# A third score bank for batch 0, its bias added by TensorE, and one maximum per bank

## The chip, the cores and the metric

The kernel runs on one core of a Trainium2 chip. The metric is device time in microseconds (us) from the start to the end of one execution. The core's engines are TensorE (PE, with its weight loads shown apart as PEld), VectorE (DVE), ScalarE (ACT), GpSimd (POOL) and SyncE (SP), whose queue issues all the DMAs here.

## The reference, cut to what matters

Three layers follow one another for 4 batches of 576 positions: windowed attention with a distance bias, and two gated layers with short convolutions. The change touches only the scores, the bias and the maximum of the attention.

```python
def _attn_ref(q, k, v):                      # 4 batches, 8 heads, 576 positions, 64 wide
    scores = scale * np.matmul(q, k.transpose(0, 1, 3, 2))
    rel = pos[:, None] - pos[None, :]
    bias = slopes[:, None, None] * (-np.abs(rel).astype(np.float32))[None, :, :]
    mask = (rel >= 0) & (rel < window)       # window 128
    scores = np.where(mask, scores + bias[None], -1000000000.0)
    scores = scores - np.max(scores, axis=-1, keepdims=True)
    attn = np.exp(scores)
    attn = attn / (np.sum(attn, axis=-1, keepdims=True) + 1e-09)
    return np.matmul(attn, v).astype(np.float32)

h = np.maximum(x @ w_in, 0.0)                # first gated layer
...
return (h * gate @ w_out)
...
val = x @ w_val                              # second gated layer
return (gate * val @ w_out)
```

## The kernel before

**Work units.** Each batch is cut into two units, u = 0 (positions 0 to 255) and u = 1 (256 to 575). For a unit the four head pairs p go through `attention`, and then `hidden` (weights `win`), `mixed` (`wout`), `valued` (`wval`) and `output` (`wo`) follow on all of the unit's columns. Every weight is kept as a high and a low part, and a dense product is three matmuls (L691, L692, L693).

**Attention of one pair.** Its query blocks of 64 positions are taken in groups of two (u = 1 ends with a group of one). A group owns one bank of the ring `pss`. TensorE writes the scores (L546); VectorE, per block, adds the bias `bm` in place, scales by -0.125 and keeps the minimum (L550, a custom instruction and a second one that reads its accumulator); ScalarE takes exp with that minimum as bias (L558) and its sum; POOL or VectorE adds 1e-9 to the sum (L561, L563), VectorE takes the reciprocal (L568). In batch 0 (`TURN = 1`) a diagonal matrix `dg` is then made (L576, L577), TensorE transposes and scales the exponentials with it back into the same bank (L584), ScalarE and VectorE copy them out in a high and a low half (L590, L592), and only then is the bank free. The product with v goes to the one bank `psx` (L651) and is copied out to x (L667, L672). `vscale` uses `psx` too (L464, L478).

**Banks.** `pss` has three banks, but `ps_s.spare = (20,)` keeps the third out of the ring for its first 20 groups, which are exactly batch 0's (4 x 2 and 4 x 3). In that time the third bank takes the fillers.

**Weights.** The four weights come in 24 pieces of 128 x 512, in the order in, out, val, o2, through a ring of three raw buffers. A piece costs two passes of ScalarE (L390, L392), two of VectorE (L394, L403), a cast by ScalarE or POOL (L409, L410) and a subtraction by POOL (L368). All of it runs in the first 100 us, beside batch 0's attention.

**Order.** A planner places all operations on the engines by priorities and assumed costs, seven passes, and keeps the shortest; engines then run their lists strictly in that order. So a change of a cost or of a ring changes the order of everything behind it. Where the plan leaves TensorE free for over 250 ns, `warm` puts fillers (L858), bf16 matmuls of zeros, until the plan's first use of the third `pss` bank.

Of the kernel before, what the change touches and what calls it, by code (L numbers as in the profile page):

```python
# [11 lines left out]
BF16 = mybir.dt.bfloat16  # L12
# [12 lines left out]
RAWS = 3  # L25
TURN = 1
RW = 2 * WC

# [216 lines left out]
def attention_moe_moe_kernel(  # L245
# [25 lines left out]
    def st(name, shape, dt):  # L271
        return sb.tile(shape, dt, name=name)
# [20 lines left out]
    bm = st("bm", [128, NP, 192], BF16)  # L293
    idle = st("idle", [128, 256], BF16)

# [24 lines left out]
    ps_s = Ring("pss", 3, [128, 512], F32, ps)  # L320
    ps_s.spare = (20,)
    ring_pw = Ring("pm", 0, None, None)
# [167 lines left out]
    def attention(b, u, p, prio, step):  # L490
# [44 lines left out]
        for gi, g in enumerate(groups):  # L535
# [8 lines left out]

            def scores(blk=blk):
                return [nc.tensor.matmul(out=o, lhsT=q_t[:, i, :], rhs=k_t[:, kc:kc + nkey], start=True, stop=True,  # L546
                                         skip_group_check=True) for i, o, nkey, kc in blk]
            pg.add("PE", sum(mm4_t(b_[2]) for b_ in blk), scores, pr, (qk,), ((sk, 0), (sk, 1)))
            for i, s, nkey, _ in blk:
                pg.add("DVE", 128 + 1.05 * nkey, lambda i=i, s=s, nkey=nkey: nc.vector.tensor_tensor_reduce(  # L550
                    out=s, in0=s, in1=bm[:, p, 192 - nkey:192], op0=ALU.add, op1=ALU.min,
                    scale=-0.125, scalar=3.0e38, accum_out=stt[:, 0, i:i + 1]), pr, ("bm",), ((sk, i - a), (stk, 0, i)), bank=sk)
            for i, s, nkey, _ in blk:
                to, tok = s, ()
                if turn:
                    c0 = 256 * i + 128 * (j0 + i < 2) + 64 * ((j0 + i) % 2 and j0 + i > 1)
                    to, tok = pe_[:, c0:c0 + nkey], ((pk, 0, i),)
                pg.add("ACT", act_t(nkey, True, 2), lambda i=i, s=s, to=to: nc.scalar.activation(  # L558
                    out=to, in_=s, func=AF.Exp, scale=-1.0, bias=stt[:, 0, i:i + 1],
                    accum_out=stt[:, 1, i:i + 1]), pr, ((stk, 0, i), "pz" + pk[1:]), ((sk, i - a), (stk, 1, i)) + tok, bank=sk)  # L560
# [236 lines left out]
    def zeros(wide, prio):  # L797

        for i, t in enumerate(ring_p.t):
            flat = t.rearrange("p q a c -> p (q a c)").bitcast(F32) if wide else t.rearrange("p q a c -> p q (a c)")  # L800
            for a, e in ((192, 384), (704, 832), (1216, 1280)):
                z = flat[:, a:e] if wide else flat[:, :, a:e]
                pg.add("POOL", 60 + (e - a) * 1.7, lambda z=z: nc.gpsimd.memset(z, 0.0), prio, (),
                       (f"pz{i}",) + tuple((f"p{i}", q, g) for q in range(2) for g in range(5)))

    zeros(TURN > 0, -1e6)
    for i, t in enumerate(ring_sg.t):
        pg.add("DVE", 200, lambda t=t: nc.vector.memset(t, 0), -2e6, (), (f"sg{i}",))
    sync(lambda: nc.sync.dma_start(out=eye, in_=ident), -1e6, (), ("eye",), 182.0)
    pg.add("POOL", 200, lambda: nc.gpsimd.memset(one, 1.0), -1e6, (), ("one",))  # L810
# [32 lines left out]
    for i, (b, u) in enumerate(todo):  # L843
# [3 lines left out]
        if i + 1 < len(todo):  # L847
# [5 lines left out]
            attentions(b2, u2, base + (9588.0 if (b, u) == (0, 0) else 0.0), t - base)  # L853
    order = pg.order()
    def warm(t, end):

        while t + 250.0 < end:
            nc.tensor.matmul(out=ps_s.t[-1][:, 0:256], lhsT=idle[:, 0:128], rhs=idle, start=True, stop=True,  # L858
                             skip_group_check=True)
            t += 125.0 if t > 940.0 + 3600.0 else 220.0  # L860

    first = next((o.start for o in order if o.eng == "PE" and any(k[0] == ps_s.name + "2" for k in o.wkeys)), 0.0)
# [68 lines left out]
```

## Time and profile before

| | |
|---|---|
| Time before, median of 3 runs | 455.79 us (453.82 to 456.14) |
| The profiled execution's own time | 454.31 us |
| Its span in the trace | 452.5 us |
| TensorE busy | 436.9 us, 97% |
| VectorE, ScalarE, POOL busy | 342.7, 319.9 and 201.9 us |
| DMA | 57.85 MB, mean 128 GB/s |

Busy times are sums over instructions, and instructions of one engine can overlap; fillers count as busy for TensorE. The time of an execution is some 1.8 us longer than the span of its trace. The share of the whole hides two stages: before about 90 us the weights are made ready and fillers run, and behind it there are none.

### The profile page before, as it was taken

The page shows a single profiled execution, that of the slowest core. Times are in us where ns is not written, and L with a number is a line of the kernel's source. Part 1 is how long each engine was busy: PE and PEld are TensorE (multiplying, and loading weights), DVE is VectorE, ACT ScalarE, POOL GpSimd, SP SyncE. Part 2 cuts the span into 40 slices and gives each one's busy share as a digit, 9 for nine tenths or more (in the row PEclk, how much of TensorE's full clock was granted, in tenths as well). Part 3 has the DMA queues.
Part 4 walks back from the last instruction along what each step waited for, and adds up shares of the span by engine and source line. Part 5 has one row for each costly group of instructions (what it writes and reads, how often), then busy time and mean ns, then how long its engine had stood idle before and what let it go on. Part 6 is the DMA issues. An engine that isn't in the chain of part 4 may idle for free.

```text
span 452.5 us, 10277 instructions
## 1 busy us (share of the span) xinstructions
PE 436.9 (97%) x3605; PEld 412.1 (91%) x3605; DVE 342.7 (76%) x1056; ACT 319.9 (71%) x930; POOL 201.9 (45%) x341
## 2 busy tenths in 40 slices
PE   7988999999999999999999999999999999999997
PEld 5667888899999999999999999998999998998996
DVE  5799988998977558995969479967979487917390
ACT  2799999964867668785974578677956576847442
POOL 1477898881553327030560436041722164454511
PEclk9999999999999999999999999999999999999999
DMA  8665757557264525658441527395352429350001
GB/s 268 221 233 198 236 171 236 178 183 250 81 100 99 129 67 114 163 128 173 132 81 49 110 77 134 103 189 138 63 112 67 128 64 170 90 119 1 0 1 59
DMA packets 75235, 57.85 MB, mean 128 GB/s; under 512 B 55984, under 2 KB 65968, under 8 KB 75184
## 3 DMA queue, kind: packets, MB, share of 16 engines
q1 hardware_dynamic: 75184, 57.21, 48.6%
q8 instruction: 28, 0.46, 0.4%
q14 instruction: 23, 0.19, 0.1%
HBM read 39.10 MB, written 4.72 MB: 97 GB/s over the span
## 4 chain that ended last, share of the span: by engine, by line
PE 59%; DVE 15%; ACT 13%; DMA 7%; issue 4%; POOL 1%; SPq 0%; DVEq 0%; ACTq 0%; POOLq 0%
PE pm L691 17%; PE pm L692 15%; PE pm L693 15%; PE pss L546 5%; DVE gts L353 4%; PE psx L651 4%; DMA pt<-p 3%; DVE t L353 2%; ACT sg L390 2%; DMA raw<-in_w_in 2%; DVE pss L550 1%; ACT pss L558 1%; PE pss L584 1%; ACT pm L392 1%; DMA raw<-in_w_val 1%
## 5 line engine op out<-in xcount | busy, mean ns | idle before, releaser
L691 PE MATMUL pm<-x,win 128*128 128x256 f32 (+1 forms) x256 | 80.9, 316 | 2.1 <-DVE t L353 2.0
L691 PE MATMUL pm<-g,wout 128*128 128x254 f32 (+1 forms) x256 | 79.8, 312 | 0.2
L692 PE MATMUL pm<-g,wout 128*128 128x254 f32 (+1 forms) x256 | 76.1, 297 | 0.0
L692 PE MATMUL pm<-x,win 128*128 128x256 f32 (+1 forms) x256 | 76.0, 297 | 0.0
L693 PE MATMUL pm<-x,win 128*128 128x256 f32 (+1 forms) x256 | 75.8, 296 | 0.0
L693 PE MATMUL pm<-g,wout 128*128 128x254 f32 (+1 forms) x256 | 75.7, 296 | 0.0
L353 DVE SCALAR_TENSOR_TENSOR t<-pm,cc,t 128x325 f32<-128x325 f32 (+3 forms) x112 | 56.1, 513 | 15.1 <-ACT t L346 11.9
L368 POOL TENSOR_TENSOR g<-t,g 128x254 fp32r<-128x254 f32 (+1 forms) x64 | 51.9, 814 | 28.2 <-ACT g L337 25.5
L546 PE MATMUL pss<-qk 128*128 128x192 f32 (+2 forms) x288 | 57.5, 322 | 3.9 <-DVE pt L592 3.0
L550 DVE CUSTOM_DVE_ANT_0 pss<-pss,bm 128x192 f32<-128x192 f32 (+2 forms) x144 | 47.9, 339 | 14.9 <-PE pss L546 12.9
L563 POOL TENSOR_SCALAR st<-st 128x2 f32<-128x2 f32 (+1 forms) x56 | 11.1, 199 | 103.6 <-ACT pss L558 87.8
L353 DVE SCALAR_TENSOR_TENSOR gts<-pm,cc,gts 128x322 f32<-128x322 f32 (+4 forms) x120 | 57.2, 506 | 0.1
L558 ACT ACTIVATE pss<-pss,st 128x192 f32<-128x192 f32 (+2 forms) x108 | 40.7, 377 | 17.2 <-DVE st L550 15.8
L691 PEld LDWEIGHTS pm<-x,win 128*128 128x128 f32 x256 | 48.2, 188 | 5.0 <-DVE t L353 3.4
L546 PEld LDWEIGHTS pss<-qk 128*128 128x128 f32 x288 | 44.3, 192 | 7.4 <-DVE pt L592 5.7
L691 PEld LDWEIGHTS pm<-g,wout 128*128 128x128 f32 x256 | 48.2, 188 | 1.6 <-ACT pm L392 0.3
L692 PEld LDWEIGHTS pm<-g,wout 128*128 128x128 f32 x256 | 48.5, 190 | 0.0
L693 PEld LDWEIGHTS pm<-g,wout 128*128 128x128 f32 x256 | 48.5, 190 | 0.0
L692 PEld LDWEIGHTS pm<-x,win 128*128 128x128 f32 x256 | 48.3, 189 | 0.0
L693 PEld LDWEIGHTS pm<-x,win 128*128 128x128 f32 x256 | 48.2, 188 | 0.0
L611 DVE SCALAR_TENSOR_TENSOR p<-pss,st,p 128x192 f16<-128x192 f32 (+1 forms) x103 | 36.4, 386 | 12.8 <-DMA pt<-p 9.0
L609 ACT ACTIVATE p<-pss,st 128x192 f16<-128x192 f32 (+1 forms) x103 | 35.9, 403 | 14.0 <-DMA pt<-p 10.2
(109 smaller groups left out, 1172.4 us busy)
## 6 DMA issues: line engine op xcount, KB each, us to landing
qk<-in_qk SPq DMA_DIRECT2D x16, 544.0 KB, 3.7
qk<-in_qk SPq DMA_DIRECT2D x16, 384.0 KB, 3.5
raw<-in_w_out SPq DMA_DIRECT2D x12, 512.0 KB, 4.0
vr<-in_vN SPq DMA_DIRECT2D x16, 256.0 KB, 3.0
raw<-in_w_in SPq DMA_DIRECT2D x8, 512.0 KB, 3.9
raw<-in_vN SPq DMA_DIRECT2D x8, 384.0 KB, 4.4
out<-t SPq DMA_DIRECT2D x16, 161.0 KB, 1.9
raw<-in_w_val SPq DMA_DIRECT2D x4, 512.0 KB, 3.5
```

The lines of the kernel that those rows point to most:

```text
L353: pg.add("DVE", dve_t(n, 0 if isinstance(scalar, float) else 1), lambda: nc.vector.scalar_tensor_tensor(out=out, in0=in0, scalar=scalar, i ...
L368: "POOL": (pool_t(n, True), lambda: nc.gpsimd.tensor_tensor(out=lo, in0=src, in1=hi.bitcast(F32), op=ALU.subtract))}
L546: return [nc.tensor.matmul(out=o, lhsT=q_t[:, i, :], rhs=k_t[:, kc:kc + nkey], start=True, stop=True, skip_group_check=True) for i, o, nke ...
L550: pg.add("DVE", 128 + 1.05 * nkey, lambda i=i, s=s, nkey=nkey: nc.vector.tensor_tensor_reduce(out=s, in0=s, in1=bm[:, p, 192 - nkey:192], ...
L558: pg.add("ACT", act_t(nkey, True, 2), lambda i=i, s=s, to=to: nc.scalar.activation(out=to, in_=s, func=AF.Exp, scale=-1.0, bias=stt[:, 0, ...
L563: "POOL": (165, lambda a=a, e=e: nc.gpsimd.tensor_scalar(stt[:, 2, a:e], stt[:, 1, a:e], 1e-9, 1.0 / PSC, op0=ALU.add, op1=ALU.mult))}
L609: pg.add("ACT", act_t(nkey, True, 1), lambda i=i, s=s, hi=hi: nc.scalar.activation(out=hi, in_=s, func=AF.Copy, scale=stt[:, 2, i:i + 1]), ...
L611: pg.add("DVE", dve_t(nkey, 1), lambda i=i, s=s, hi=hi, lo=lo: nc.vector.scalar_tensor_tensor(out=lo, in0=s, scalar=stt[:, 2, i:i + 1], in ...
L651: r.append(nc.tensor.matmul(out=oap, lhsT=lhs, rhs=rhs, start=(i == first[h]), stop=(i == last[h]), skip_group_check=True))
L691: return [nc.tensor.matmul(out=o, lhsT=wh, rhs=hi, start=first, stop=False), nc.tensor.matmul(out=o, lhsT=wh, rhs=lo, start=False, stop=Fa ...
L692: nc.tensor.matmul(out=o, lhsT=wh, rhs=lo, start=False, stop=False),
L693: nc.tensor.matmul(out=o, lhsT=wl, rhs=hi, start=False, stop=last)]
```

## The change

Batch 0 (`BIASED`) gets the third score bank. TensorE adds the bias itself: behind each score matmul one of the bf16 identity `eyeb` with `bm`, into the same columns. VectorE takes one maximum over a group's bank (two when its blocks differ in width), and a tiny instruction on VectorE or POOL multiplies it by -0.125. `eyeb` is a copy of `eye` by ScalarE. The fillers, now 192 columns wide, go to columns 320 to 511 of `psx`, and accumulate there; they are placed up to 80 us of the plan.

```diff
+FILL = 80000.0
+BIASED = (0,)
...
-    idle = st("idle", [128, 256], BF16)
+    idle = st("idle", [128, 128], BF16)
+    eyeb = st("eyeb", [128, 128], BF16)
...
-    ps_s.spare = (20,)
...
+                for i, o, nkey, kc in blk:
+                    r.append(nc.tensor.matmul(out=o, lhsT=q_t[:, i, :], rhs=k_t[:, kc:kc + nkey], start=True, stop=not biased,
+                                              skip_group_check=True))
+                    if biased:
+                        r.append(nc.tensor.matmul(out=o, lhsT=eyeb, rhs=bm[:, p, 192 - nkey:192], start=False, stop=True,
+                                                  skip_group_check=True))
...
+            pg.add("PE", sum(mm4_t(b_[2]) + biased * (30 + b_[2] / 2.4) for b_ in blk), scores, pr,
+                   (qk,) + (("bm", "eyeb") if biased else ()), ((sk, 0), (sk, 1)))
+            if biased:
+                same = len({nkey for _, _, nkey, _ in blk}) == 1
+                for bs in ([blk] if same else [[x] for x in blk]):
...
+                    pg.add("DVE", 68 + 1.1 * nkey * nbl, lambda src=src, i0=i0, nbl=nbl: nc.vector.tensor_reduce(
+                        out=stt[:, 0, i0:i0 + nbl], in_=src, axis=mybir.AxisListType.X, op=ALU.max), pr,
+                        ((sk, 0), (sk, 1)), ((stk, 3, i0),), bank=sk)
+                pg.add(("DVE", "POOL"), (75, 165), (
+                    lambda a=a, e=e: nc.vector.tensor_scalar(stt[:, 0, a:e], stt[:, 0, a:e], -0.125, 0.0, op0=ALU.mult, op1=ALU.add),
...
-            for i, s, nkey, _ in blk:
+            for i, s, nkey, _ in () if biased else blk:
...
+    sync(lambda: nc.sync.dma_start(out=eye, in_=ident), -1e6, (), ("eye",), 182.0)
     zeros(TURN > 0, -1e6)
+    pg.add("ACT", 220, lambda: nc.scalar.activation(out=eyeb, in_=eye, func=AF.Copy), -1e6, ("eye",), ("eyeb",))
...
         while t + 250.0 < end:
-            nc.tensor.matmul(out=ps_s.t[-1][:, 0:256], lhsT=idle[:, 0:128], rhs=idle, start=True, stop=True,
+            nc.tensor.matmul(out=ps_x.t[0][:, 320:512], lhsT=idle[:, 0:128], rhs=bass.AP(idle.tensor, idle.offset, [list(idle.ap[0]), [0, 2], [1, 96]]), start=not filled, stop=True,
                              skip_group_check=True)
...
-                if o.start < first:
+                if o.start < FILL:
```

The program's first scores on TensorE, before (`qk` holds a pair's queries and keys, `idle` the zeros of the fillers):

```order
L546 MATMUL pss_125<-qk_105 128x64
L546 MATMUL pss_125<-qk_105 128x128
L546 MATMUL pss_126<-qk_105 128x192 x2
L858 LDWEIGHTS idle
L858 MATMUL pss_127<-idle 128x256
```

and in the changed kernel, whose lines have moved by a few numbers:

```order
L552 MATMUL pss_126<-qk_106 128x64
L555 LDWEIGHTS eyeb
L555 MATMUL pss_126<-bm,eyeb 128x64
L552 MATMUL pss_126<-qk_106 128x128
L555 LDWEIGHTS eyeb
L555 MATMUL pss_126<-bm,eyeb 128x128
L552 MATMUL pss_127<-qk_106 128x192
```

Each score block has a weight load and a matmul behind it, 36 times in all. A little further on in the changed kernel, with what an instruction waits for:

```order
L466 MATMUL psx_129<-eye,vmx 4x128 [waits DMAHW2_49,Pool_49]
L607 MATMUL pss_126<-dg_117,p_116 128x128 [waits Activation_49,Pool_49]
L607 MATMUL pss_126<-dg_118,p_116 128x128 [waits DVE_49]
L886 LDWEIGHTS idle
L886 MATMUL psx_129<-idle 128x192 [waits DVE_49]
L886 LDWEIGHTS idle
L886 MATMUL psx_129<-idle 128x192
```

The first of this block of eleven fillers now waits for VectorE, which reads `psx` behind L466; before, fillers waited for nothing but `idle`. There are six such blocks, with 57 of the 121 fillers. The third place is the last dense work ahead of the first matmul with `wo`, before (`wval` is the weight of `valued`, `g` its moving operand):

```order
L584 MATMUL pss_126<-dg_117,p_115 128x128 x2
L584 MATMUL pss_126<-dg_118,p_115 128x128 x2
L691 MATMUL pm_122<-g_87,wval_65 128x254
L692 MATMUL pm_122<-g_87,wval_65 128x254
L693 MATMUL pm_122<-g_87,wval_66 128x254
```

and in the changed kernel:

```order
L714 MATMUL pm_123<-g_80,wval_65 128x254
L715 MATMUL pm_123<-g_80,wval_65 128x254
L716 MATMUL pm_123<-g_80,wval_66 128x254
L552 MATMUL pss_126<-qk_106 128x64
L552 MATMUL pss_126<-qk_106 128x128
L714 MATMUL pm_123<-g_88,wval_65 128x254
```

Before, batch 0's transposes still stand there; in the changed kernel they are done, and scores of batch 1 stand in their place.

## Rows read from the trace of the kernel before

**Rows 1.** The page: span, and busy time of each engine.
```profile
span 452.5 us, 10277 instructions
PE 436.9 (97%) x3605; PEld 412.1 (91%) x3605; DVE 342.7 (76%) x1056; ACT 319.9 (71%) x930; POOL 201.9 (45%) x341
```

**Rows 2.** Five stretches: length, busy us of each engine, PE clock, DMA share, GB/s.
```profile
0.00:15.00 15.00, 12.00 (x81) 9.74 (x82) 9.32 (x36) 4.93 (x18) 2.81 (x15) 1.00 0.77 256
15.00:30.00 15.00, 12.84 (x110) 9.84 (x109) 11.61 (x37) 13.71 (x39) 10.42 (x18) 1.00 0.69 223
30.00:75.00 45.00, 41.73 (x351) 35.56 (x348) 42.02 (x113) 42.81 (x108) 38.29 (x56) 1.00 0.64 209
75.00:90.00 15.00, 14.39 (x142) 13.73 (x140) 13.69 (x36) 14.77 (x37) 13.31 (x18) 1.00 0.61 202
90.00:452.50 362.50, 355.89 (x2930) 343.27 (x2930) 266.02 (x837) 243.69 (x732) 137.10 (x237) 1.00 0.45 105
```

**Rows 3.** Stretches again, the fillers (L858) alone: PE, PEld, clock.
```profile
0.00:30.00 30.00, 13.08 (x93) 9.36 (x93) 1.00 0.73 240
30.00:75.00 45.00, 11.86 (x96) 9.03 (x93) 1.00 0.64 209
```

**Rows 4.** Waits up to 95 us: total us, times, longest.
```profile
PEld pss L546 <- DVE pt L592: 5.7, 10, 1.6
```

**Rows 5.** Timeline near the start: start, duration, engine, line.
```profile
1.66 0.42 SPq L809 DMA_DIRECT2D eye<-in_ident  x1
...
5.56 0.23 DVE L550 CUSTOM_DVE_ANT_0 pss<-pss,bm 128x64 f32<-128x64 f32 x1 [3.48 <-PE pss L546]
```

**Rows 6.** VectorE's groups by shape up to 100 us: busy us, mean ns.
```profile
L550 DVE CUSTOM_DVE_ANT_0 pss<-pss,bm 128x192 f32<-128x192 f32 x27 | 9.7, 358 | 0.3
L550 DVE DVE_READ_ACCUMULATOR2_ANT st<- 128x1 f32 x35 | 4.9, 141 | 0.0
L444 DVE TENSOR_REDUCE vmx<-raw 128x2 f32<-128x768 f32 x3 | 2.8, 936 | 0.0
L444 DVE TENSOR_REDUCE vmx<-gts 128x4 f32<-128x1024 f32 x1 | 1.2, 1219 | 0.3 <-DMA gts<-in_vN 0.3
L466 DVE TENSOR_REDUCE vst<-psx 4x1 f32<-4x128 f32 x2 | 0.5, 272 | 0.0
```

**Rows 7.** Timeline of VectorE from 24 us, one group's blocks and the next.
```profile
24.11 0.35 DVE L550 CUSTOM_DVE_ANT_0 pss<-pss,bm 128x192 f32<-128x192 f32 x1
...
24.84 0.26 DVE L550 CUSTOM_DVE_ANT_0 pss<-pss,bm 128x64 f32<-128x64 f32 x1
...
25.41 0.68 DVE L403 SCALAR_TENSOR_TENSOR gts<-raw,pm 128x512 uint32<-128x512 uint32 x1
```

**Rows 8.** Timeline of TensorE, twelve fillers in a row.
```profile
25.16 1.48 PE L858 MATMUL pss<-idle 128*128 128x256 bf16 x12
```

**Rows 9.** ScalarE's groups by shape up to 100 us.
```profile
L558 ACT ACTIVATE p<-pss,st 128x192 f32<-128x192 f32 x27 | 11.1, 418 | 1.5 <-DVE st L550 1.5
L590 ACT ACTIVATE pt<-pss 128x512 f16<-128x512 f32 x11 | 6.5, 594 | 3.5 <-PE pss L584 3.5
L409 ACT ACTIVATE wo<-gts 128x512 fp32r<-128x512 f32 x3 | 1.9, 631 | 0.1
```

**Rows 10.** Timeline: the last piece of `wo` on POOL, its first matmul on TensorE.
```profile
97.43 1.28 POOL L368 TENSOR_TENSOR wo<-gts,wo 128x512 fp32r<-128x512 f32 x1
...
99.48 0.28 PE L691 MATMUL pm<-g,wo 128*128 128x254 f32 x1
```

**Rows 11.** Timeline of TensorE: transposes, scores and products with v one behind another.
```profile
88.43 0.61 PE L584 MATMUL pss<-dg,p 128*128 128x128 f32 x4
...
88.87 0.61 PE L546 MATMUL pss<-qk 128*128 128x64 f32 x4
...
89.99 0.92 PE L546 MATMUL pss<-qk 128*128 128x192 f32 x4 [0.51 <-DVE pt L592]
...
90.84 0.76 PE L651 MATMUL psx<-pt,v 128*64 128x128 f16 x20
...
91.53 0.19 PEld L691 LDWEIGHTS pm<-g,wval 128*128 128x128 f32 x1
```

More of the change, by code (lines that the diff above doesn't have):

```diff
@@ L543, in attention @@
                 blk.append((i, gp[:, 192 * (i - a):192 * (i - a) + nkey], nkey, 64 * (max(0, j - 2) - k0)))
[L545 to L548, printed above, removed]
-            for i, s, nkey, _ in blk:
+            biased = b in BIASED
@@ new lines, in scores @@
+            def scores(blk=blk, biased=biased):
+                r = []
+                for i, o, nkey, kc in blk:
[4 more added lines that the diff above has]
+                                                  skip_group_check=True))
+                return r
@@ new lines, in attention @@
+            pg.add("PE", sum(mm4_t(b_[2]) + biased * (30 + b_[2] / 2.4) for b_ in blk), scores, pr,
[3 more added lines that the diff above has]
+                for bs in ([blk] if same else [[x] for x in blk]):
+                    i0, nkey, nbl = bs[0][0], bs[0][2], len(bs)
+                    src = gp[:, 192 * (i0 - a):192 * (i0 - a) + 192 * nbl].rearrange("p (i c) -> p i c", c=192)[:, :, 0:nkey]
+                    pg.add("DVE", 68 + 1.1 * nkey * nbl, lambda src=src, i0=i0, nbl=nbl: nc.vector.tensor_reduce(
[3 more added lines that the diff above has]
+                    lambda a=a, e=e: nc.vector.tensor_scalar(stt[:, 0, a:e], stt[:, 0, a:e], -0.125, 0.0, op0=ALU.mult, op1=ALU.add),
+                    lambda a=a, e=e: nc.gpsimd.tensor_scalar(stt[:, 0, a:e], stt[:, 0, a:e], -0.125, 0.0, op0=ALU.mult, op1=ALU.add)),
+                    pr, tuple((stk, 3, x[0]) for x in blk if (not same or x[0] == a)), tuple((stk, 0, i) for i in g))
@@ L558, in attention @@
                 pg.add("ACT", act_t(nkey, True, 2), lambda i=i, s=s, to=to: nc.scalar.activation(
-                    out=to, in_=s, func=AF.Exp, scale=-1.0, bias=stt[:, 0, i:i + 1],
+                    out=to, in_=s, func=AF.Exp, scale=0.125 if biased else -1.0, bias=stt[:, 0, i:i + 1],
                     accum_out=stt[:, 1, i:i + 1]), pr, ((stk, 0, i), "pz" + pk[1:]), ((sk, i - a), (stk, 1, i)) + tok, bank=sk)
@@ L804, in zeros @@
                        (f"pz{i}",) + tuple((f"p{i}", q, g) for q in range(2) for g in range(5)))
+    sync(lambda: nc.sync.dma_start(out=eye, in_=ident), -1e6, (), ("eye",), 182.0)
     zeros(TURN > 0, -1e6)
+    pg.add("ACT", 220, lambda: nc.scalar.activation(out=eyeb, in_=eye, func=AF.Copy), -1e6, ("eye",), ("eyeb",))
     for i, t in enumerate(ring_sg.t):
         pg.add("DVE", 200, lambda t=t: nc.vector.memset(t, 0), -2e6, (), (f"sg{i}",))
-    sync(lambda: nc.sync.dma_start(out=eye, in_=ident), -1e6, (), ("eye",), 182.0)
     pg.add("POOL", 200, lambda: nc.gpsimd.memset(one, 1.0), -1e6, (), ("one",))
@@ L854, in attention_moe_moe_kernel @@
     order = pg.order()
+    filled = []
     def warm(t, end):
         while t + 250.0 < end:
-            nc.tensor.matmul(out=ps_s.t[-1][:, 0:256], lhsT=idle[:, 0:128], rhs=idle, start=True, stop=True,
+            nc.tensor.matmul(out=ps_x.t[0][:, 320:512], lhsT=idle[:, 0:128], rhs=bass.AP(idle.tensor, idle.offset, [list(idle.ap[0]), [0, 2], [1, 96]]), start=not filled, stop=True,
                              skip_group_check=True)
+            filled.append(1)
             t += 125.0 if t > 940.0 + 3600.0 else 220.0
-    first = next((o.start for o in order if o.eng == "PE" and any(k[0] == ps_s.name + "2" for k in o.wkeys)), 0.0)
     pe = None
```

## The prediction

> **What bounds the kernel now.** I read the page first: TensorE is busy 436.9 of 452.5 us [rows 1], so it looks like the bound everywhere. The view by stretches says where it is not. Behind 90 us it is busy 355.89 of 362.5 us [rows 2]: that stage is full, 6.6 us short of all of it. Ahead of 75 us it is busy 66.57 of 75 us (12.00 + 12.84 + 41.73), but the same stretches for the fillers alone take 13.08 and 11.86 us [rows 3]. So of the first 75 us TensorE is idle for 8.4 and fills for 24.9: 33.3 us in which no result is made. In that stage the others are the bound: from 30 to 75 us ScalarE is busy 42.81, VectorE 42.02 and POOL 38.29 of 45 us [rows 2], with the weights and batch 0's attention. In the first 15 us none of them is: ScalarE 4.93, VectorE 9.32, POOL 2.81. There the attention goes round in two banks; the waits say that TensorE's scores waited ten times, 5.7 us, for VectorE to copy the transposed exponentials out and free a bank [rows 4].
>
> Where does the first stage end? Output's weight `wo` is the last to be made ready. Its last piece ends on POOL at 98.71 us (97.43 + 1.28), and 0.8 us later, at 99.48, the first matmul with it starts [rows 10]. From then on TensorE never again lacks weights. So the end is this moment plus all work that TensorE has left at it. A change in the first stage pays in two ways: that moment comes earlier, or more useful work has been done ahead of it.
>
> **The change part by part.**
>
> *The maximum.* Before, a group of two blocks of 192 held VectorE from 24.11 to 24.84, 0.73 us, and one of 64 and 128 from 24.84 to 25.41, 0.57 us [rows 7]. One block of 192 is half of the first, 0.37 us. The trace has no maximum over 2 x 192 in a bank. The nearest rows are L444's, 936 ns for 768 and 1219 for 1024 elements: 1.105 ns an element and 87 ns besides, so an estimate of 0.51 us for 384, 0.30 for 192, 0.23 for 128 and 0.16 for 64. L466 reads 128 from a bank in 272 ns [rows 6], 43 ns above this line. I take 0.53, 0.32, and 0.41 for the two narrow ones together. Twelve wide groups save 0.20 each, four narrow ones 0.16, four single blocks 0.05: 3.2 us. Of the twenty small multiplications by -0.125 five stand on VectorE in the order; at the 0.14 us of an accumulator read [rows 6] they take 0.7 back. VectorE gains 2.5 us. The bounds are 1.5 (43 ns more on each of the 24 maxima) and about 6, if a block of 192 is charged its 0.358 + 0.141 us without overlap [rows 6]: 0.47 saved in each of twelve wide groups. [...]
>
> *The path through a group gets longer.* The first exp waited for one block's half; now it waits for the bias matmul, the maximum of both blocks and the multiplication, some 0.5 us more per group. With a third bank this is hidden: three groups are under way where there were two.
>
> *The bias on TensorE.* 36 loads and matmuls of up to 192 columns. Nearest row: twelve fillers, each a load and a matmul of 256 bf16 columns, in 1.48 us [rows 8], 0.123 us each; scaled by columns 0.093. So 3.3 to 4.4 us, all ahead of the first `wo` matmul, in the stage with 33.3 us of slack: nothing in the sum, and up to 4.4 if that cover were gone.
>
> *The start.* The bias matmul needs the copy of `eye`, which was issued at 1.66 us, while the first minimum began at 5.56 [rows 5]. That leaves 3.9 us for landing and copying. I take nothing; bound 0.5 us.
>
> *Useful work ahead of the first `wo` matmul.* I counted the orders of both kernels up to it. Dense matmuls: 240 in both. Scores: 37 blocks before, 46 now. Transposes: 58 and 64. Products with v: 138 and 168. The trace prices them: two wide score blocks take 0.85 us (89.99 to 90.84), two transposes four instructions, 0.44 us (88.43 to 88.87), twenty products 0.69 us (90.84 to 91.53) [rows 11]. The nine score blocks are of mixed width, so 0.35 rather than 0.42 each: 3.2 us. Six transposes at 0.22: 1.3 us. Thirty products at 0.035: 1.0 us. That is 5.5 us of work that no longer lies behind.
>
> *When that moment comes.* More attention ahead of the last piece means more for ScalarE ahead of it. Up to the last piece's two passes the order now has 8 more exponentials, 3 more copies to `pt`, 2 more copies to `p`, and 3 fewer casts of weights, which moved to POOL; the rest cancels. At 0.418, 0.594, 0.418 and 0.631 us [rows 9] that is 3.3 + 1.8 + 0.8 - 1.9 = 4.0 us more. If all of it is on the path, the first `wo` matmul comes 4.0 us later; if it fits in what is now idle, no later at all. In the first 30 us ScalarE is idle for 11.4 us [rows 2], about half of it with the first loads under way, and the third bank and VectorE's 2.5 us work on just that stretch. I take 1.5 us.
>
> **The sum.** 5.5 - 1.5 = 4.0 us. On the profiled execution's 454.3 us this gives 450.3. The median of the runs shown is 1.5 us above it, 455.8, so the forecast is 451.8 us. With both ends of the lateness: 450.3 (not late) to 454.3 (all of it).
>
> **Rivals.**
>
> *No change.* ScalarE is 95% busy from 30 to 75 us [rows 2] and its work ahead of the last weight grows by 4.0 us. If also the bias' wait for `eye` and the longer path cost a microsecond, 0.5 us of gain is left: 455.3. Against it: ScalarE's idle 11.4 us early on, and the ten waits for a bank.
>
> *Fillers come late (the other side).* The fillers write `psx`, and in six blocks the first waits until VectorE or ScalarE has read `psx`. A block that starts late runs in full ahead of a real matmul that may be ready. The 57 fillers of those blocks at 0.1 us are 5.7 us. If all of it shows, 451.8 + 5.7 = 457.5. It decides against the change from 4.0 us on, that is if seven in ten of these fillers stand in front of ready work. For it: in-order queues. Against it: where I followed the lists, the next real matmul behind such a block waits for an instruction that stands several places further down the same VectorE queue.
>
> [...]
>
> **How the numbers follow.** About 0.5% (2.3 us) is what a measurement of this kernel can tell from no change. The likeliest case, 450.3 to 454.3, has a chance of 0.55, most of it (0.44) below 453.5. No change: 0.22. Late fillers: 0.10. The clock: 0.06. Better than 450 (part of the 6.6 us that TensorE lacks behind 90 us also closes, as the order there is new): 0.07. So faster 0.51, same 0.33, slower 0.16. The range reaches from 448.5, half of that closed, to 457.5, the late fillers in full; the likeliest case's own is 450 to 454.5.
>
> **What would show it.** After: the first matmul with `wo` between 98 and 102 us, with fillers below 13 us in total; the wide maximum at 0.50 to 0.56 us; the waits of scores for L592's successor well under 5.7 us; ScalarE's busy time in the first 15 us above 4.93; granted clock 1.00; TensorE short of the stretch from 100 us on by no more than 7 us. Wrong if the first `wo` matmul comes after 104 us (weights too late), if TensorE waits for the readers of `psx` (late fillers), or if TensorE idles more behind 100 us, where it had 6.6 us left.

## The result and the profile after

The changed kernel takes 448.08 us (median of 4 runs, 446.88 to 450.06) against 454.95 for the kernel before (4 runs, 453.82 to 456.14): ratio 0.9853, 95% interval 0.9806 to 0.990. Forecast were 451.8 us, 4.0 below before, and a range of 448.5 to 457.5: the direction was right, but the gain of 6.9 us is 1.7 times the one forecast, and the time lies 0.4 us below the range.

The profiled execution was the longest of the changed kernel's, 450.06 us. The page of the changed kernel, to be set beside [rows 1]:

```profile
span 448.3 us, 10172 instructions
...
PE 431.5 (96%) x3569; PEld 410.0 (91%) x3569; DVE 341.4 (76%) x1012; ACT 316.7 (71%) x924; POOL 208.2 (46%) x364
```

Its stretches, as in [rows 2]:

```profile
0.00:15.00 15.00, 12.48 (x60) 10.36 (x61) 7.25 (x23) 4.53 (x17) 3.40 (x18) 1.00 0.71 239
15.00:30.00 15.00, 13.62 (x128) 11.11 (x128) 13.03 (x37) 13.95 (x42) 10.85 (x23) 1.00 0.75 233
30.00:75.00 45.00, 40.52 (x352) 36.08 (x350) 42.58 (x100) 40.79 (x107) 39.79 (x67) 1.00 0.61 201
75.00:90.00 15.00, 13.33 (x143) 12.41 (x143) 14.11 (x39) 14.29 (x36) 12.32 (x21) 1.00 0.56 186
90.00:448.30 358.30, 351.58 (x2895) 340.00 (x2892) 264.43 (x817) 243.16 (x726) 141.89 (x238) 1.00 0.45 109
```

VectorE's groups up to 100 us: the new maximum, and the small multiplication where it fell to VectorE.

```profile
L565 DVE TENSOR_REDUCE st<-pss 128x2 f32<-128x384 f32 x12 | 6.5, 544 | 1.2 <-PE pss L555 1.2
L569 DVE TENSOR_SCALAR st<-st 128x2 f32<-128x2 f32 x4 | 2.3, 566 | 0.0
```

And the waits up to 95 us, of scores for a bank, which answer to [rows 4], and of fillers for a reader of `psx`:

```profile
PEld pss L552 <- DVE pt L615: 2.1, 3, 0.9
...
PE psx L886 <- ACT t L690: 1.4, 2, 0.9
PE psx L886 <- DVE x L697: 1.1, 1, 1.1
...
PE psx L886 <- DVE vsc L484: 0.3, 1, 0.3
```

The wide maximum takes 0.544 us (0.53 was taken), and scores wait for a bank 2.1 us where it was 5.7.

**Where the time came from.** The last work counts, so the span is split at the first matmul with `wo`, as the forecast did it. This row of the changed kernel and, in the fence behind it, that of a second profile of the same program (run e1 below) give the moment:

```profile
102.77 0.28 PE L714 MATMUL pm<-g,wo 128*128 128x254 f32 x1
```

```profile
99.97 0.28 PE L714 MATMUL pm<-g,wo 128*128 128x254 f32 x1
```

The stretch from there to the end, in the kernel before (from 99.5), in the changed kernel and in its second profile (columns as in [rows 2]):

```profile
99.50:452.50 353.00, 346.39 (x2838) 334.21 (x2836) 256.62 (x811) 235.78 (x709) 129.78 (x227) 1.00 0.45 104
```

```profile
102.80:448.30 345.50, 339.79 (x2778) 328.97 (x2776) 252.18 (x784) 231.08 (x692) 129.82 (x223) 1.00 0.44 104
```

```profile
100.00:445.30 345.30, 339.89 (x2778) 329.02 (x2776) 251.95 (x784) 231.35 (x692) 130.05 (x223) 1.00 0.43 104
```

The stretch is 353.0 us before and 345.5 and 345.3 after: 7.5 and 7.7 us shorter. TensorE has 6.6 and 6.5 us less to do in it, and it idles for 5.7 and 5.4 us where it was 6.6. The moment itself comes 3.3 us later in the first profile and 0.5 in the second. So the spans fall by 7.5 - 3.3 = 4.2 and by 7.7 - 0.5 = 7.2 us. The median's gain of 6.9 is nearer to the second.

The same stretch for single lines: before, the scores (L546), the products (L651) and batch 0's transposes (L584); after, the scores (L552) and the products (L674). The first number behind the length is TensorE's busy time:

```profile
99.50:452.50 353.00, 41.78 (x214) 1.00 0.45 104
99.50:452.50 353.00, 22.14 (x534) 1.00 0.45 104
99.50:452.50 353.00, 1.90 (x12) 1.00 0.45 104
```

```profile
102.80:448.30 345.50, 38.16 (x196) 1.00 0.44 104
102.80:448.30 345.50, 21.04 (x504) 1.00 0.44 104
```

Eighteen score instructions (nine blocks) less are 3.6 us, thirty products 1.1. The twelve transpose instructions that stood there, 1.9 us, are gone. Together 6.6 us, which is what TensorE's busy time lost.

### The profile page after: what moved, and what is told of

It reads as the page before. It is cut to its first block, busy times and chain, and to the rows that moved or that the text cites. A ratio compares the mean times of both kernels' runs of the same rounds, so it can differ in the third digit from the quotient of the medians.

```text
span 448.3 us, 10172 instructions
## 1 busy us (share of the span) xinstructions
PE 431.5 (96%) x3569; PEld 410.0 (91%) x3569; DVE 341.4 (76%) x1012; ACT 316.7 (71%) x924; POOL 208.2 (46%) x364
## 4 chain that ended last, share of the span: by engine, by line
PE 57%; DVE 14%; ACT 8%; DMA 5%; POOL 2%; issue 1%; SPq 0%; DVEq 0%; ACTq 0%; POOLq 0%
PE pm L714 17%; PE pm L715 16%; PE pm L716 16%; PE pss L552 5%; DVE gts L355 4%; PE psx L674 3%; DVE t L355 2%; DMA vr<-in_vN 2%; DMA pt<-p 2%; DMA raw<-in_w_out 1%; ACT pss L581 1%; DVE pss L573 1%; DVE p L634 1%; DVE g L778 1%; ACT t L348 1%
## 5 line engine op out<-in xcount | busy, mean ns | idle before, releaser
L355 DVE SCALAR_TENSOR_TENSOR t<-pm,cc,t 128x254 f32<-128x254 f32 (+3 forms) x112 | 56.1, 513 | 16.4 <-ACT t L348 13.1
L370 POOL TENSOR_TENSOR g<-t,g 128x254 fp32r<-128x254 f32 (+1 forms) x64 | 52.0, 815 | 31.3 <-ACT g L339 28.7
L552 PE MATMUL pss<-qk 128*128 128x192 f32 (+2 forms) x288 | 61.0, 332 | 2.5 <-DVE pt L615 1.4
L355 DVE SCALAR_TENSOR_TENSOR gts<-pm,cc,gts 128x322 f32<-128x322 f32 (+4 forms) x120 | 58.2, 510 | 2.9 <-ACT g L775 2.7
L581 ACT ACTIVATE pss<-pss,st 128x192 f32<-128x192 f32 (+1 forms) x108 | 41.0, 380 | 17.0 <-DVE st L573 14.9
L552 PEld LDWEIGHTS pss<-qk 128*128 128x128 f32 x288 | 45.7, 197 | 5.9 <-DVE pt L615 2.1
L573 DVE CUSTOM_DVE_ANT_0 pss<-pss,bm 128x192 f32<-128x192 f32 (+1 forms) x108 | 35.8, 343 | 8.7 <-PE pss L552 7.8
```

What stands on the lines that cost most here:

```text
L355: pg.add("DVE", dve_t(n, 0 if isinstance(scalar, float) else 1), lambda: nc.vector.scalar_tensor_tensor(out=out, in0=in0, scalar=scalar, i ...
L370: "POOL": (pool_t(n, True), lambda: nc.gpsimd.tensor_tensor(out=lo, in0=src, in1=hi.bitcast(F32), op=ALU.subtract))}
L552: r.append(nc.tensor.matmul(out=o, lhsT=q_t[:, i, :], rhs=k_t[:, kc:kc + nkey], start=True, stop=not biased, skip_group_check=True))
```

## Why two executions of one program differ by 2.9 us

In the first profile the first dense matmul (`win`) starts at 30.1 us, in the second at 27.7, and all behind it is shifted by about as much. Eleven fillers, in the first and in the second profile (TensorE's timeline):

```profile
11.05 1.97 PE L886 MATMUL psx<-idle 128*128 128x192 bf16 x11
```

```profile
9.99 1.07 PE L886 MATMUL psx<-idle 128*128 128x192 bf16 x11
```

0.179 us each, and 0.097. In the first profile all matmuls take nearly twice as long until some 15 us, in the second until some 6. The column of the granted clock says 1.00 for both. But the trace's list of clock levels has its first entry, the upper level, at 14.87 us in the first profile and at 6.12 in the second, and where the list has no entry the column counts the clock as full. Single matmuls tell what the level was. Bias matmuls of 192 columns, in the first profile ahead of its first entry and behind it, and in the kernel of e8, where the clock is on record as 0.50 at that time:

```profile
14.36 0.37 PE L555 MATMUL pss<-bm,eyeb 128*128 128x192 bf16 x1
...
18.67 0.25 PE L555 MATMUL pss<-bm,eyeb 128*128 128x192 bf16 x1
```

```profile
14.95 0.37 PE L555 MATMUL pss<-bm,eyeb 128*128 128x192 bf16 x1
```

The clock of e8 in rows of two us each:

```profile
8.00:10.00 2.00, 1.17 (x8) 0.69 (x8) 1.79 (x4) 0.00 (x0) 0.75 (x3) 0.85 1.07 394
10.00:12.00 2.00, 2.00 (x10) 1.41 (x8) 1.68 (x8) 1.44 (x7) 0.50 (x3) 0.50 0.51 196
```

There TensorE had waited 1.9 us for the second pair's queries and keys, until 8.83 us; in the second row the clock is 0.50, the lower level, and it stays there until about 16 us. In all 18 profiles single fillers and bias matmuls take 1.2 to 1.6 times their usual length ahead of the list's first entry, which comes between 4.8 and 14.9 us, and the usual length behind it, wherever the list has the upper level. So by these lengths the slow start is at the lower level, and an execution's mean clock, which counts it as full, does not show it. It lasts until 15 us in one of the two profiles and 6 in the other; why is not shown.

## The experiments

The kernel before was run beside each; its median was 454.7 to 455.2 us on the chips used. Ratios are to it, with 95% intervals. This table has what the profiles show of the kernels below: start of the first dense matmul, of the first `wo` matmul, length of the stretch behind it and TensorE's idle time in it (us), and the median time of all runs.

| kernel | first dense | first `wo` | behind it | idle there | time |
|---|---|---|---|---|---|
| before | 33.2 | 99.5 | 353.0 | 6.6 | 454.95 |
| changed | 30.1 | 102.8 | 345.5 | 5.7 | 448.08 |
| e1, again | 27.7 | 100.0 | 345.3 | 5.4 | 448.58 |
| e2, bank only | 32.5 | 99.6 | 348.5 | 8.1 | 449.63 |
| e3, bias only | 32.8 | 105.8 | 346.5 | 4.8 | 456.45 |
| e4, 16 fillers | 27.2 | 98.3 | 347.6 | 7.0 | 450.66 |
| e5, half bank | 35.0 | 107.6 | 349.2 | 8.9 | 457.89 |
| e6, before, order 2 | 32.3 | 102.6 | 349.4 | 6.7 | 453.84 |
| e7, changed, order 2 | 27.8 | 99.1 | 344.2 | 5.1 | 447.05 |
| e8, bias in batch 1 too | 34.6 | 102.6 | 349.8 | 6.2 | 455.03 |
| e9, half bank, 34 fillers | 32.8 | 106.4 | 349.8 | 9.3 | 458.76 |
| e10, 12 fillers more | 27.2 | 99.4 | 345.4 | 5.3 | 447.33 |
| e11, both of e7 and e10 | 27.4 | 99.6 | 345.2 | 5.7 | 446.64 |
| e12, no fillers | 27.5 | 98.7 | 345.4 | 5.2 | 448.87 |
| e13, bank only, order 2 | 26.8 | 105.7 | 344.4 | 5.5 | 449.40 |
| e14, bias only, order 2 | 37.5 | 111.8 | 350.3 | 7.1 | 462.58 |
| e15, half bank, order 2 | 33.6 | 102.7 | 345.0 | 4.7 | 449.18 |
| e16, changed, order 3 | 26.3 | 99.3 | 347.9 | 7.0 | 451.22 |

### The change taken apart (e1 to e4)

**e1** is the changed kernel once more, with no edit.

> The changed kernel once more, unaltered. Theory A (the first stage does more useful work ahead of the first matmul with wo, and the size was mis-set): 447 to 449 us, 6 to 8 us below before, first matmul with wo at 101 to 104 us as in the profile of the changed kernel. Theory B (the true gain is the 4 us of the sum, and the runs shown drew a high before and a low after): 450 to 452 us.

Measured: 448.58 us (6 runs, 447.12 to 449.84), ratio 0.9859 [0.9832, 0.9885]. The gain is there again, 6.2 us, as theory A has it, though the first `wo` matmul comes earlier, at 100.0 us, than it says.

**e2** has the third bank and the fillers in `psx`, but the old addition, scaling and minimum on VectorE:

```diff
-BIASED = (0,)
+BIASED = ()
```

> Batch 0 keeps VectorE's own bias and minimum, and has the third score bank and the new fillers: the bias matmuls and the single maximum are left out. If the third bank makes the gain: 448 to 451 us, at least 4 us below before. If VectorE's shorter maximum makes it: 453.5 to 456 us. My sum gave VectorE 2.5 of the relief and the bank the rest, so I lean to 450.

Measured: 449.63 us (4 runs), ratio 0.9882 [0.9854, 0.9910]. The third bank gives 5.1 of e1's 6.2 us.

**e3** is the other half: bias by TensorE and the wide maximum, with two banks, and fillers in the third:

```diff
+    ps_s.spare = (20,)
...
-            nc.tensor.matmul(out=ps_x.t[0][:, 320:512], lhsT=idle[:, 0:128], ...
+            nc.tensor.matmul(out=ps_s.t[-1][:, 0:192], lhsT=idle[:, 0:128], ...
```

> Batch 0 has TensorE's bias and the single maximum per bank, but only two score banks, with the fillers in the third as before. If the third bank makes the gain: 454 to 457 us, for the path through a group is longer by about 0.5 us and only two groups are under way. If VectorE's relief makes it: 449 to 452 us.

Measured: 456.45 us (12 runs, 453.66 to 458.57), ratio 1.0032 [1.0007, 1.0057]: slower, as expected if the third bank makes the gain. The stretch behind the first `wo` matmul is 6.5 us shorter than before (4.7 us less work for TensorE, 1.8 less idle time), but that matmul comes 6.3 us later in the profile. Nine of the twelve executions have a mean clock of 0.991 to 0.996; the other three took 454.08, 455.14 and 455.28 us, so a part of the loss goes with the lower clock. Waits of its transposes and scores up to 106 us:

```profile
PEld pss L608 <- POOL dg L601: 5.4, 7, 2.0
...
PE pss L608 <- POOL dg L601: 3.5, 4, 1.8
PEld pss L553 <- DVE pt L616: 3.1, 7, 0.7
```

In the kernel before, the transposes' two waits for POOL's diagonal were 3.3 and 1.9 us. That the path through a group (score, bias, maximum, multiplication, exp, sum, diagonal), which grew by two steps, is what two banks no longer hide fits these rows; it is argued, not shown.

**e4** keeps the sixteen fillers at the start and leaves out the other 105, and with them all waits of fillers for readers of `psx`:

```diff
-                if o.start < FILL:
+                if o.start < FILL and not unread:
```

> The changed kernel with the sixteen fillers ahead of its first scores alone; the 105 behind them, and with these all six waits of fillers for a reader of psx, are left out. If late fillers cost something: 1 to 5 us below the changed kernel, clock still 1.00. If fillers keep the clock: the granted clock falls in the first 90 us, and the time is 3 to 10 us above the changed kernel. If neither: within 1 us of it.

Measured: 450.66 us (7 runs, 447.57 to 453.47), ratio 0.9903 [0.9869, 0.9937]. The mean granted clock of its seven executions was 1.000 in those of 447.57, 447.71 and 450.66 us, and 0.988 to 0.992 in the four of 449.26 to 453.47. Without the late fillers the shortest execution is no shorter than the changed kernel's (446.88), and more of them show a lower clock and are longer. The median is 2.1 to 2.6 us above the changed kernel's, between the expectations; the intervals overlap, and e12 below, with no fillers at all, takes 448.87 us.

### How much is the order's (e5 to e9)

**e5** gives the third bank to ten of the twenty groups, otherwise as e2:

```diff
+    ps_s.spare = (10,)
```

> The third bank is kept out of the ring for the first ten of batch 0's twenty groups and given to the other ten; no bias matmul, no wide maximum. Theory W (what pays is useful TensorE work done ahead of the first wo matmul, less the lateness of that moment): the order has 44 score blocks, 64 transposes and 168 products with v ahead of it, against 37, 58 and 138 before and 46, 64 and 168 with the third bank throughout. Priced by rows of before that is 2.45 + 1.3 + 1.0 = 4.8 us of the 5.5, so nearly the whole gain of the third bank: 449.6 to 450.8, the first wo matmul between 98 and 102 us. Rival D (the gain goes with the number of groups that have the third bank, since each saves its wait): half of the 5.1 us, 452.2.

Measured: 457.89 us (6 runs, 455.93 to 460.14), ratio 1.0074 [1.0046, 1.0102], clock 0.985 to 0.996. Both expectations fail. Three us at a time, and TensorE's timeline:

```profile
24.00:27.00 3.00, 0.84 (x14) 0.57 (x14) 2.84 (x10) 3.00 (x12) 2.76 (x6) 0.82 0.97 318
27.00:30.00 3.00, 1.48 (x10) 1.37 (x10) 3.00 (x8) 2.68 (x6) 1.68 (x2) 0.50 0.83 288
30.00:33.00 3.00, 3.00 (x20) 2.83 (x19) 0.11 (x1) 0.00 (x0) 0.00 (x0) 0.54 0.58 202
```

```profile
28.52 3.84 PE L887 MATMUL psx<-idle 128*128 128x192 bf16 x23 [3.67 <-ACT t L691]
32.15 0.93 PE L608 MATMUL pss<-dg,p 128*128 128x128 f32 x4
```

The rival of the late fillers is here in full. 23 fillers wait until ScalarE has read `psx` (at 28.5 us), the clock has meanwhile fallen to 0.50, they take 0.167 us each (0.097 at the upper level, above), and the transposes, whose diagonal was ready at 28.7, start at 32.15. From 30 to 33 us VectorE, ScalarE and POOL stand still, because all of them wait for TensorE.

**e9** is the same order without the fillers that wait (the edit of e4 on e5).

> The half bank again (third bank for ten of batch 0's twenty groups), with the same order of all useful work, but only those fillers that wait for no reader of psx: 34 in place of 162. In the trace of the half bank 23 fillers waited for ScalarE from 24.9 to 28.5 us, then ran until 32.2 at a granted clock of 0.50 to 0.54, while VectorE, ScalarE and POOL stood still for 4.2 to 4.5 us. Theory F (late fillers and the clock that falls in their wait made that kernel 7 us slower than its count of early work says): 449.5 to 452, the first wo matmul near 101. Rival O (its order is bad whatever the fillers do): 456 to 458. Rival K (fewer fillers, so the clock falls elsewhere): 453 to 456 with a granted clock under 0.99.

Measured: 458.76 us (6 runs, 455.70 to 459.57), ratio 1.0068 [1.0045, 1.0091], clock 0.972 to 0.978. The theory that the late fillers cost 7 us falls. Without them the transposes do start at 28.52 us in place of 32.15, so in that place the fillers cost 3.6 us. But TensorE waits until then all the same (3.88 us, for ScalarE), the clock falls there too (0.62 and 0.50 below), to a mean of 0.978, and of what was won 1.2 us are left at the first `wo` matmul (106.4 against 107.6) and none in the median:

```profile
27.00:30.00 3.00, 1.48 (x6) 1.51 (x7) 3.00 (x9) 2.73 (x6) 1.88 (x3) 0.62 0.73 186
30.00:33.00 3.00, 3.00 (x19) 2.46 (x18) 1.29 (x4) 1.50 (x3) 2.26 (x4) 0.50 0.86 305
```

So the gap is the order's. Fillers in it hold up the work behind them, by 3.6 us in that place; without them the mean clock is lower, 0.972 to 0.978 against 0.985 to 0.996.

**e6** and **e7** change nothing but one assumed cost of the planner by 4 ns, in the kernel before and in the changed one. Every instruction stays, but for some fillers in e6 (181 where there were 193), and some small ones change between POOL and VectorE. In e6 the order is another from early on. In e7 it is so on TensorE from 147 us, on the other engines from 85 us; ahead of that it is the changed kernel's:

```diff
-                pg.add("DVE", 128 + 1.05 * nkey, lambda i=i, s=s, nkey=nkey: nc.vector.tensor_tensor_reduce(
+                pg.add("DVE", 124 + 1.05 * nkey, lambda i=i, s=s, nkey=nkey: nc.vector.tensor_tensor_reduce(
```

> The kernel before with one assumed cost of the planner changed by 4 ns (124 instead of 128 in the custom minimum); every instruction and bank stays, only the order is another. It has 38 score blocks, 64 transposes and 158 products with v ahead of the first wo matmul against 37, 58 and 138. Theory W: 0.35 + 1.3 + 0.7 = 2.4 us earlier if that moment is not late, so 452.4, and up to 454.8 if it is as much later. Rival R (the time of the whole tells orders apart only by luck, whatever stands ahead of wo): as likely above 454.8 as below, by up to 3 us. If the time stays within 1 us of before, an order's luck is small and the change's 6 us are the third bank's.

Measured: 453.84 us (12 runs, 452.94 to 456.89), ratio 0.9988 [0.9970, 1.0006]. Behind the first `wo` matmul 3.6 us less, and that matmul 3.1 us later: both terms of the sum are there, and cancel.

> The changed kernel with the same assumed cost changed by 4 ns, for batches 1 to 3, which alone still use the custom minimum. The counts ahead of the first wo matmul are those of the changed kernel (46, 64, 168). Theory W: within 1.5 us of it, 447.1 to 450.1, since the first stage is as before and only the full stage behind has another order. Rival R: the 2 us by which the change gave more than forecast came from a lucky order behind wo; then this one falls back to 450.5 to 452, with 6 to 7 us of idle TensorE behind the first wo matmul where the changed kernel had 5.4.

Measured: 447.05 us (6 runs, 445.07 to 449.32), ratio 0.9837 [0.9809, 0.9866], TensorE's idle time behind the first `wo` matmul 5.1 us. So the gain is not that of a lucky order behind the first `wo` matmul. For another order ahead of it see e16.

**e8** has bias and wide maximum in batch 1 too, whose attention lies in the full stage:

```diff
-BIASED = (0,)
+BIASED = (0, 1)
```

> Bias by TensorE and the wide maximum in batch 1 as well, whose attention lies behind 90 us, where TensorE has no slack. 36 more bias matmuls, 28 of them behind the first wo matmul. Theory C (on TensorE's bound stage each costs its 0.093 to 0.123 us): 2.6 to 3.4 us more than the changed kernel, 451.2 to 452.0, and TensorE's busy time behind 90 us up by as much. Rival H (they fit into waits, or VectorE's relief pays for them): 448.0 to 449.5, as the changed kernel.

Measured: 455.03 us (12 runs, 452.56 to 458.69), ratio 1.0012 [0.9988, 1.0035]: above both expectations, the whole gain is lost. Its profile is 7.1 us longer than e1's. Behind the first `wo` matmul TensorE is busy 343.6 us, 3.7 more than in e1; two score blocks more stand there, some 0.8 us, and 28 bias matmuls, so 0.10 us each, within the price of the forecast (0.093 to 0.123), which was to be paid if the cover were gone. It idles there 0.8 us more. The other 2.6 us lie ahead of the `wo` matmul, at 102.6 against 100.0; the doubled matmuls of this execution (above) are part of them.

### The start and the fillers (e10 to e12)

**e10** puts twelve fillers ahead of the second pair's scores, where TensorE waits for the pair's load:

```diff
+                if npe == 2:
+                    warm(5000.0, 5000.0 + 12 * 125.0 + 200.0)
+                npe += 1
                 if o.start < FILL:
```

> The changed kernel with twelve more fillers ahead of the second pair's scores, where TensorE waited 0.5 to 1.9 us for the pair's queries and keys; they wait for nothing. Theory S (the times of the changed kernel spread over 446.9 to 450.1 because in some executions TensorE's matmuls take twice as long until about 17 us): with no gap there the slow ones go, 446.5 to 447.8 at the median, and the spread falls below 1.5 us. Rival N (the slow stretch begins at the start, whatever follows): median and spread as the changed kernel, 448.1 to 449, or up to 0.7 us more for fillers that run into ready scores.

Measured: 447.33 us (4 runs, 445.96 to 448.11), ratio 0.9823 [0.9804, 0.9843], clock 1.000 in all. **e11** has this and the order of e7.

> The changed kernel with both: the other order (one assumed cost of the planner 4 ns less) and the twelve fillers. Where both help, it is the fastest so far: 444.8 to 446.2 by theory S, with no run above 447.5. By rival N it is the other order alone, 446.5 to 447.5 with runs up to 449.

Measured: 446.64 us (5 runs, 445.26 to 446.84), ratio 0.9805 [0.9789, 0.9822], clock 0.999 or more in all. The twelve fillers, and that they run into nothing, in e10:

```profile
6.49 1.15 PE L886 MATMUL psx<-idle 128*128 128x192 bf16 x12
8.06 0.32 PE L552 MATMUL pss<-qk 128*128 128x64 f32 x1 [0.41 <-DMA qk<-in_qk]
```

None of these nine executions is above 448.11 us, where five of the ten of the changed kernel are (448.19 to 450.06). That the gap is what makes the slow start last is not shown by this, and the traces speak against it. In the profiles of e10 and e11 the upper level begins at 5.4 and 5.1 us, ahead of the twelve fillers. In the first profile of the changed kernel the matmuls are slow before the gap already, and its gap is shorter than the one in the second:

```profile
8.14 0.69 PE L552 MATMUL pss<-qk 128*128 128x64 f32 x2 [0.45 <-DMA qk<-in_qk]
```

```profile
8.30 0.43 PE L552 MATMUL pss<-qk 128*128 128x64 f32 x2 [1.04 <-DMA qk<-in_qk]
```

The median of e10 is where theory S has it, but the medians' intervals overlap, and the spread (2.2 us) is wider than expected. The median of e11 is the fastest measured here, but lies where rival N has it; only its longest run, 446.84, is as theory S says.

**e12** has no fillers at all (`FILL = 0.0`).

> The changed kernel without any filler. Theory C (the granted clock falls when TensorE has little to do ahead of 90 us, and fillers hold it up): a clock under 0.98 in most runs and 452 to 458, the first dense matmul later than 33 us. Rival U (useful work alone holds it up, and fillers only stand in the way): 446.5 to 449, clock 0.99 or more. The kernel with sixteen fillers alone lay between, 450.7 with its runs from 447.6 to 453.5.

Measured: 448.87 us (6 runs, 445.83 to 451.19), ratio 0.9860 [0.9829, 0.9892], clock 0.991 to 1.000. In time and clock it is the rival's: without any filler the mean clock is 0.991 to 1.000, and the median is 0.8 us above the changed kernel's 448.08, with intervals that overlap. What fillers buy shows at most in the spread, 5.4 us without them, 3.2 in the ten executions of the changed kernel, 2.2 in e10 and 1.6 in e11, from four to ten executions each.

### Second orders of the parts (e13 to e16)

e5 and e15 show why an edit in one order proves little. **e13**, **e14** and **e15** are e2, e3 and e5 with the edit of e6; **e16** is the changed kernel with 132 in place of 128.

> The third bank alone (no bias matmul, no wide maximum) in a second order: one assumed cost of the planner 4 ns less. It has 46 score blocks, 64 transposes and 168 products with v ahead of the first wo matmul, as in the first order. Theory W (early work less lateness, the bank gives the early work in any order): 448 to 451, as the first order's 449.6. Rival R (the first order was lucky): above 452, the first wo matmul later than 103 us.

Measured: 449.40 us (4 runs, 447.44 to 452.01), ratio 0.9885 [0.9845, 0.9925]: the gain of the bank alone is there in this order too. The profiled one was the longest, with its first `wo` matmul at 105.7 us and a granted clock of 0.77 from 90 to 105 us.

> Bias by TensorE and the wide maximum alone, two banks, in a second order. 40 score blocks, 64 transposes and 138 products with v stand ahead of the first wo matmul (40, 64, 158 in the first order). Theory W: 1.05 + 1.3 = 2.4 us of early work, less a lateness that was 6 us in the first order. If two banks and the longer path make it late in any order: 455 to 458. Rival R (the 6 us were that order's): 451 to 454.

Measured: 462.58 us (4 runs, 461.04 to 463.84), ratio 1.0170 [1.0143, 1.0197]: above both expectations and worse still than the first order, the first `wo` matmul 12.3 us late.

> The third bank for ten of twenty groups in a second order; 42 score blocks, 64 transposes and 168 products ahead of the first wo matmul. Theory R here (the first order had a gap of TensorE from 25 to 28.5 us with a clock of 0.50 behind it, and that is an order's accident): 450 to 453 with a clock of 0.99 or more. Rival H (half a bank is worse than none in any order): 455 to 459 with a clock under 0.99 again.

Measured: 449.18 us (4 runs, 448.24 to 450.37), ratio 0.9878 [0.9857, 0.9899], clock 1.000. The same three us as in e5 have no gap:

```profile
27.00:30.00 3.00, 2.92 (x30) 2.66 (x28) 2.46 (x9) 2.63 (x9) 2.46 (x5) 1.00 0.93 328
```

Half a bank is 3 us slower than before in one order and 6 us faster in the other: its 8.7 us between them are the order's.

> The whole change in a third order (the same assumed cost 4 ns more); 46, 64 and 168 ahead of the first wo matmul, 101 fillers. Theory W: 446 to 450, the stretch behind the first wo matmul 344 to 347 us. Rival R (the orders differ by more than the change gives): below 445 or above 452.

Measured: 451.22 us (7 runs, 448.94 to 453.63), ratio 0.9915 [0.9884, 0.9945], clock 0.991 to 0.996. Between the two expectations, faster than before by 4.0 us, so over three orders the change gains 4.0 to 7.7 us. Of these only e16 has another order from early on: that the whole change gains in more than one order ahead of the first `wo` matmul rests on it alone. Its profile has the lower level too, in the stretch behind the last filler:

```profile
90.00:105.00 15.00, 14.36 (x102) 13.80 (x103) 13.56 (x42) 10.19 (x32) 9.96 (x15) 0.89 0.73 201
```

## Where the prediction was right, and where its gain was too small

**The frame held.** TensorE's busy time behind the first `wo` matmul goes by what stands ahead of it in the order: 346.4 us with 37 score blocks, 58 transposes and 138 products (before), 342.7 with 38, 64 and 158 (e6), 341.7 with 40, 64 and 158 (e3), and 338.9 to 340.9 with 46, 64 and 168 (the changed kernel and e2, in all their orders). The half bank's two orders, with 44 and 42 blocks, lie within this range (340.2 and 340.4), so the count is good to about a microsecond.

**The failed step: useful work ahead of the first `wo` matmul.** It was put at 5.5 us; the stretch behind that moment became 7.5 to 7.7 us shorter. Half of the miss is price: the nine score blocks were worth 3.6 us (3.2 forecast), the six transposes 1.9 (1.3), the thirty products 1.1 (1.0). The forecast took its prices from short pieces of one timeline [rows 11]. Means over the whole stretch of the same trace, shown above, are 41.78 / 107 = 0.39 us a block, 1.90 / 6 = 0.32 a transpose and 22.14 / 534 = 0.041 a product: 3.5 + 1.9 + 1.2 = 6.6 us, which is what came.

The other half is 0.9 to 1.2 us of TensorE's idle time behind that moment, which the sum left as it was and only a rival of 0.07 let close. Over all orders it is 4.7 to 9.3 us, in five profiles of the changed kernel's own order 5.2 to 7.0 (changed, e1, e4, e10, e12), so it is no sure part of the change. Lateness, 0.5 us where 1.5 were taken, makes up the rest of the second profile's 7.2 us. That the first profile's 4.2 is next to the sum's 4.0 is luck: the stretch is 2.0 us shorter than forecast, and its start 1.8 us later.

**When that moment comes.** 1.5 us of lateness were forecast, with bounds of 0 and 4.0. It was 3.3 us in the first profile and 0.5 in the second; some 2.4 of the 3.3 are the slow matmuls of its first 15 us, which put it, at 102.8 us, beyond the 98 to 102 named, and which also fit ScalarE's 4.53 us in the first 15, where over 4.93 was expected (5.84 in e1). The size was within the bounds, but the reason is not confirmed: the bounds were ScalarE's work, while over the other kernels the moment lies anywhere between 98.3 and 111.8 us, with an order's gaps and the clock.

**The start** was put at nothing, with a bound of 0.5 us: in the second profile the first bias matmul waits 0.34 us for `eyeb`, in the first not at all.

**The third bank and VectorE.** The forecast let bank and relief work together. Apart, the bank alone gains 5.1 and 5.8 us in two orders. Bias and maximum alone lose 1.7 and 7.4. On top of the bank they gain 1.0 and 1.9 us in the two pairs of like edits (e2 and e1, e13 and e7, each to its own runs of before), but the intervals of either pair overlap, and e7's order is new only behind the first `wo` matmul, e13's from early on. The path that got longer was said to be hidden by the third bank; the losses of e3 and e14, without it, fit that. VectorE's gain of 2.5 us was overstated: the wide maximum's price was right, but all maxima together took 9.9 us where 9.3 were taken, and the five small multiplications 2.4 in place of 0.7 (0.566 us for each of two elements, not 0.14). That leaves some 0.2 us.

**The rivals.** *No change* did not come. *Late fillers*: the changed kernel's fillers waited 2.8 us in all for readers of `psx`; in e5 one block stood 3.5 us in front of ready work, so the mechanism is real, though e4 and e9 gain nothing by removing them. *The clock*: no run shows the term behind the forecast's 0.06. What the runs showed in its place: the profile of the changed kernel has 1.00 throughout, as forecast, but its first 14.9 us, not on record, are at the lower level by the lengths of their matmuls, 8.8 us more than in the second profile, and cost some 2.4 us. The first 5.4 us of the kernel before are too (a filler takes 0.42 us in them and 0.27 behind), though the column of [rows 2] says 1.00. Later falls are on record: the executions of e4, e7 and e12 with a mean clock of 0.996 or less are, but for two, longer than their medians. In the mean they are 3.1, 2.8 and 2.9 us longer than the others of their kernel, though not in every execution. Fillers took 14.4 us in the first profile and 13.6 in the second, where under 13 were expected.

**Open.** Why the lower level lasts until 15 us in one execution and 6 in another is not settled. How much of an order's lateness is its gaps and how much the clock that falls in them was not separated. The kernel before was not run without its fillers, of which it has 193 and the changed kernel 121. That their number makes the gain is unlikely: fillers are put in after the order is fixed (the changed kernel, e4, e10 and e12 have the same order of all else in their traces), so they leave the work behind the first `wo` matmul as it is, and without any (e12) that matmul comes at 98.7 us, 1.3 us earlier than in e1. With 162 to 168 fillers e15 gains 6.0 us, and e3 and e5 lose.

## What to carry to other kernels

Split such a span at the moment from which one engine is busy almost throughout, and price what has moved across that moment by totals over the long stretch, not by short pieces of a timeline. Where a planner sets the order, judge a part of a change only in two or more orders: here an assumed cost altered by 4 ns moved one kernel by 8.7 us and others by 0.2 to 6.1. If fillers are used, let them wait for nothing and write where no other engine reads: in e5 one block waited 3.7 us and then ran for 3.6 in front of ready work. That they gain time was not shown here.

## What the runs showed of the hardware

**VectorE's small TENSOR_SCALAR of 128 x 2 elements waited for POOL's instruction, one of 128 x 1 did not.** The multiplication L569 of 128 x 2 elements took 0.15, 0.16, 0.64 and 1.31 us. VectorE's and POOL's timelines in the changed kernel:

```profile
72.32 1.31 DVE L569 TENSOR_SCALAR st<-st 128x2 f32<-128x2 f32 x1
...
81.64 0.14 DVE L584 TENSOR_SCALAR st<-st 128x1 f32<-128x1 f32 x1
```

```profile
71.07 2.54 POOL L370 TENSOR_TENSOR wout<-gts,wout 128x512 fp32r<-128x512 f32 x2
...
81.02 1.27 POOL L370 TENSOR_TENSOR wval<-gts,wval 128x512 fp32r<-128x512 f32 x1 [0.25 <-ACT wval L411]
```

The one of 1.31 us ends at 73.63 us, the second of POOL's two at 73.61; the one of 0.64 us ends at 19.60, and a POOL instruction of 0.67 us from 18.90 at 19.57. The one of 128 x 1 runs through in the midst of POOL's. Over all 18 profiles, 189 such VectorE instructions of 128 x 2 began while a POOL instruction ran that had 0.25 us or more to go: 187 ended 0.02 to 0.03 us behind it (in the kernel before and the changed one all 22, which took 0.29 to 1.31 us). All 63 of 128 x 1 ran through, in 0.13 to 0.16 us, and so did 49 of 50 of 128 x 2 that began up to 0.12 us ahead of POOL's. The reciprocal of 128 x 2 (L568, in the changed kernel L591) did not wait: in the same two profiles 44 began while a POOL instruction ran that had 0.25 us or more to go, and all ran through, in 0.15 to 0.17 us. What makes the difference is not shown.

**The granted clock's column can say 1.00 where the clock is not on record.** Until the first entry of the trace's list (14.87 us in the first profile) a filler took 0.179 us in a row of like ones, and 0.097 at the upper level. Durations of like instructions are the better witness there.
